# A padded warm-up buffer: 60 bytes that move the buffers behind it

## The chip, the cores and the metric

The kernel runs on one core of a Trainium2 chip. The metric is the device time of one launch in microseconds; times are medians of several runs. The engines of the core run beside each other: TensorE (PE, with its weight loads shown as PEld), VectorE (DVE), ScalarE (ACT), GpSimd (POOL) and SyncE (SP), which here issues nearly all DMA transfers.

## The reference, cut to what matters

Two blocks, one behind the other: a recurrent attention over 768 positions for 4 batches and 8 heads of width 64, and a gated feed-forward block on its 3072 rows.

```python
for t in range(S):                       # attention, per batch and head
    state = gamma * state + einsum('bhd,bhe->bhde', k[:, :, t], v[:, :, t])
    y[:, :, t] = scale * einsum('bhd,bhde->bhe', q[:, :, t], state)
x = y.transpose(0, 2, 1, 3).reshape(3072, 512)
g, val = x @ w_gate, x @ w_val           # 512 x 1536 each
out = (silu(g) * val) @ w_out            # 1536 x 512
```

## The kernel before

The 3072 rows are done in four segments of 768 (s = 0 to 3). Each segment has an up-projection (x times the gate and value weights) and a down-projection (times w_out). The attention that makes the next segment's x runs in pieces of small matmuls (line 766) inside the down-projection of the segment before. Every operand of the large products is split into three parts of lower precision, which VectorE, ScalarE and GpSimd write (`near_a`, `near_b`, `near_c` at lines 967, 970, 973, and `far_a` to `far_c` at 976, 979, 983; where `both` is used in place of `pool`, line 407), and the products of the parts are summed in PSUM.

The large matmuls stand at four lines, each with a weight operand (stationary, 128 x 128) and a moving operand:

- L914 and L896 (`plain_part`, `plain`): up-projection of segment 0. Weights in `oitem` tiles, moving operand x0 of 256 or 384 columns. 144 and 480 matmuls.
- L1062 (`product`, called by `up3`): up-projection of segments 1 to 3, by a scheme with seven products for eight. The weights come in groups, two in `gitem` tiles and one in an `oitem` tile; the moving operand is `xa` or `xb`, 384 columns. 1512 matmuls, six (three parts, two blocks) for each product.
- L1125 (`down`): down-projection of all segments, 12 feature blocks f in each. Stationary operand is the split hidden block `hs[f]`, a `gitem` tile; moving operand is the split w_out block `wo[f]`, an `oitem` tile, 512 columns. 864 matmuls, 18 for each f.

In L1062 and L1125 both operands of one matmul are read from on-chip memory; all matmuls write PSUM banks.

`item(kind, n)` hands out the tiles. The kind "g" has four slots used in turn (tags g0 to g3, 9216 bytes a partition), the kind "o" three (tags o0 to o2, 6144 bytes). Slot g2 is also used once for an `oitem` of segment 0. The pool lays a tag down when it is first asked for, in this order: hT, xa, xb, g0, g1, g3 (as `rawp`), loads, tmp, chunk_x, tab, local, last, states, warm, and behind them o0, o1, o2 and g2. In the built program warm starts at byte 200,960 of each partition, the o slots at 201,504, 207,648 and 213,792, and g2 at 219,936; hT, xa (x0), xb (first), g0, g1, g3, loads, tmp and chunk_x start at 16,512, 53,376, 90,240, 117,888, 127,104, 136,320, 145,536, 168,064 and 178,304.

`warm` is a buffer of 128 + 1 float32 columns. It is set to zero on VectorE (line 1229); one column of it takes a Silu on ScalarE, so that the function's table is loaded early (line 1230); and eight matmuls on its zeros (`warm_up`, line 1214) run while the first inputs are on their way. Nothing reads it afterwards.

The order of the instructions is written out by hand in the string `PLAN`: each word is one step (so `0/D3.1` is segment 0, down-projection, f = 3, output block 1), and `run` issues them in that order. Waits between engines follow from the tiles.

Of the kernel before, what the change touches and what calls it, by code (L numbers as in the profile page):

```python
# [14 lines left out]
AF = mybir.ActivationFunctionType  # L15
ALU = mybir.AluOpType

P = 128
# [358 lines left out]
def tile_retnet_swiglu(  # L377
# [13 lines left out]
    nc = tc.nc  # L391
# [17 lines left out]
    def place(name, n, dtype=F32, **kw):  # L409
        return consts.tile([P, n], dtype, name=name, **kw)  # L410
# [15 lines left out]
    local = place("local", 2 * NP * HC + H + NP)  # L426
    last = place("last", 512)
    states = consts.tile([P, 2, 2, NP, D], F32, name="states")
    warm = place("warm", P + 1)

    def lay(sizes):
        at, out = 0, []
# [778 lines left out]
    def warm_up(n):  # L1211

        for _ in range(n):
            nc.tensor.matmul(banks[3][:, :P], warm[:, :P], warm[:, :P], start=True, stop=True,
                             skip_group_check=True)
# [11 lines left out]
    for n in range(2):  # L1227
        load_chunk(n, 1, nc.scalar)
    nc.vector.memset(warm, 0.0)
    nc.scalar.activation(warm[:, P:], warm[:, :1], AF.Silu)  # L1230
    warm_up(8)
    for f in range(NF):
        up(f, T0 + UP0 * (f - NPF))
# [67 lines left out]
```

## Time and profile before

| what | value |
| --- | --- |
| runs | 657.35, 659.65, 660.76 us; median 659.65 |
| profiled execution: its span from first to last instruction | 655.4 us |
| around that span, median of the runs less the span | 4.25 us |
| TensorE, VectorE, ScalarE, GpSimd busy in the profile | 642.4, 490.1, 389.9, 270.0 us |
| L1062: matmuls, busy | 1512, 292.8 us |
| L1125: matmuls, busy | 864, 212.9 us |
| L896 and L914: matmuls, busy | 624, 104.2 us |
| granted TensorE clock | 1.00 |

The profiled execution's own time is known by its span; what lies around the span is only known from the runs. Busy times of single matmuls overlap, since they are pipelined, so the number of us that a row of n matmuls adds to the span is read from the distance of its start to the next row's start, not from its busy time. Buffer numbers are left out of the profile's names: `gitem` is any of the four slots.

### The profile page before, as it was taken

What the parts mean: (1) busy time and instruction counts of PE and PEld (TensorE: products, weight loads), DVE (VectorE), ACT (ScalarE), POOL (GpSimd) and SP (SyncE); (2) the same over time, 40 slices, a digit from 0 to 9 for tenths busy, and PEclk for the clock granted to TensorE, in tenths of its full rate; (3) what the DMA queues carried; (4) which work ended last, traced back from release to release, by engine and by line L of the source; (5) the groups of instructions that cost most, each with busy time, mean ns of one, the idle gap of its engine ahead of it and who ended that gap; (6) DMA issues with size and microseconds to landing.
All of it is one profiled execution on the core that took longest, in us unless ns stands there. A gap on an engine that the chain in (4) does not pass through costs nothing.

```text
span 655.4 us, 14042 instructions
## 1 busy us (share of the span) xinstructions
PE 642.4 (98%) x5576; PEld 582.5 (89%) x5576; DVE 490.1 (75%) x712; ACT 389.9 (59%) x860; POOL 270.0 (41%) x174
## 2 busy tenths in 40 slices
PE   7999999999999999999999999999999999999997
PEld 6899999987779999997778999998777999999886
DVE  5888688798998887675787868767498776778361
ACT  4688788577855555665766555455676554554211
POOL 1443446533445675630103765640103766562000
PEclk9999999999999999999999999999999999999999
DMA  9999897499867444177765640448677434304554
GB/s 331 372 354 337 316 347 265 165 367 282 280 206 292 162 145 170 33 225 253 235 231 209 214 141 23 164 160 294 193 247 260 165 140 169 114 0 162 184 201 146
DMA packets 50051, 140.13 MB, mean 214 GB/s; under 512 B 4929, under 2 KB 17473, under 8 KB 49985
## 3 DMA queue, kind: packets, MB, share of 16 engines
q1 hardware_dynamic: 49552, 138.57, 61.2%
q8 instruction: 44, 0.72, 0.4%
q10 hardware_dynamic: 432, 0.66, 0.3%
q14 instruction: 23, 0.18, 0.1%
HBM read 109.32 MB, written 29.88 MB: 212 GB/s over the span
## 4 chain that ended last, share of the span: by engine, by line
PE 86%; DVE 5%; DMA 3%; ACT 3%; issue 1%; POOL 1%; SPq 0%; ACTq 0%; DVEq 0%; POOLq 0%
PE bank L1062 40%; PE bank L1125 26%; PE bank L896 12%; PE bank L766 5%; PE bank L914 2%; DMA rawp<-in_w_gate_dram 1%; ACT chunk_x L996 1%; DMA hT<-in_k_n_dram 1%; DVE gitem L970 1%; DMA hT<-in_q_t_dram 1%; DVE oitem L983 1%; POOL oitem L973 1%; DVE gitem L407 0%; DVE xa L983 0%; PE bank L721 0%
## 5 line engine op out<-in xcount | busy, mean ns | idle before, releaser
L1125 PE MATMUL bank<-oitem,gitem 128*128 128x512 f32 x864 | 212.9, 400 | 2.3 <-DVE oitem L983 1.3
L1125 PEld LDWEIGHTS bank<-oitem,gitem 128*128 128x128 f32 x864 | 159.4, 188 | 41.5 <-DVE oitem L983 3.1
L973 POOL TENSOR_TENSOR gitem<-gitem 128x768 fp32r<-128x768 f32 x72 | 143.3, 1999 | 107.1 <-DVE gitem L970 102.3
L1062 PE MATMUL bank<-xa,gitem 128*128 128x384 f32 x864 | 163.0, 337 | 0.6 <-ACT tmp L1078 0.3
L1062 PEld LDWEIGHTS bank<-xa,gitem 128*128 128x128 f32 x864 | 151.3, 188 | 3.0 <-ACT tmp L1077 2.1
L973 POOL TENSOR_TENSOR oitem<-oitem 128x256 fp32r<-128x256 f32 (+1 forms) x60 | 65.8, 1102 | 72.8 <-DVE oitem L970 70.8
L970 DVE SCALAR_TENSOR_TENSOR gitem<-gitem,loads 128x768 fp32r<-128x768 f32 x72 | 80.7, 1138 | 14.1 <-ACT gitem L967 11.6
L967 ACT ACTIVATE gitem<-loads 128x768 fp32r<-128x768 f32 x72 | 59.3, 842 | 51.4 <-PE bank L1062 40.7
L896 PE MATMUL bank<-x,oitem 128*128 128x384 f32 x480 | 86.1, 340 | 0.8 <-POOL oitem L973 0.8
L896 PEld LDWEIGHTS bank<-x,oitem 128*128 128x128 f32 x480 | 84.5, 188 | 1.4 <-POOL oitem L973 1.1
L1062 PE MATMUL bank<-xb,gitem 128*128 128x384 f32 x432 | 85.5, 335 | 0.2 <-POOL gitem L973 0.2
L1062 PEld LDWEIGHTS bank<-xb,gitem 128*128 128x128 f32 x432 | 76.0, 188 | 1.1 <-POOL gitem L973 0.5
L970 DVE SCALAR_TENSOR_TENSOR gitem<-gitem,hT 128x768 fp32r<-128x768 f32 x48 | 51.0, 1067 | 28.4 <-ACT gitem L967 28.3
L967 ACT ACTIVATE gitem<-hT 128x768 fp32r<-128x768 f32 x48 | 39.9, 840 | 43.1 <-PE bank L1125 35.8
L996 ACT COPY chunk_x<-bank 64x128 f32<-64x128 f32 x144 | 35.4, 260 | 29.9 <-PE bank L766 25.4
L793 POOL TENSOR_TENSOR loads<-loads,tab 128x512 f32<-128x512 f32 x9 | 13.8, 1534 | 93.5 <-PE bank L766 93.5
L407 DVE SCALAR_TENSOR_TENSOR gitem<-gitem 128x768 fp32r<-128x768 f32 x48 | 45.9, 962 | 0.6
L1062 PE MATMUL bank<-xb,oitem 128*128 128x384 f32 x216 | 44.3, 340 | 0.0
L1062 PEld LDWEIGHTS bank<-xb,oitem 128*128 128x128 f32 x216 | 38.3, 188 | 0.4 <-POOL oitem L973 0.2
L970 DVE SCALAR_TENSOR_TENSOR oitem<-oitem,loads 128x256 fp32r<-128x256 f32 (+1 forms) x42 | 32.6, 781 | 3.8 <-ACT oitem L967 3.7
L979 POOL TENSOR_TENSOR oitem<-oitem 128x512 fp32r<-128x512 f32 x12 | 20.0, 1667 | 28.4 <-ACT oitem L976 28.4
L1079 DVE TENSOR_TENSOR hT<-bank,tmp 128x384 f32<-128x384 f32 x36 | 20.0, 554 | 15.0 <-PE bank L1062 14.8
(112 smaller groups left out, 785.0 us busy)
## 6 DMA issues: line engine op xcount, KB each, us to landing
loads<-wup SPq DMA_DIRECT2D x36, 896.0 KB, 4.8
oitem<-wdnt SPq DMA_DIRECT2D x36, 768.0 KB, 4.3
wdnt<-oitem SPq DMA_DIRECT2D x12, 768.0 KB, 4.7
wup<-first SPq DMA_DIRECT2D x9, 896.0 KB, 6.7
rawp<-in_w_gate_dram SPq DMA_DIRECT2D x12, 512.0 KB, 6.7
rawp<-in_w_val_dram SPq DMA_DIRECT2D x12, 512.0 KB, 5.9
rawp<-in_w_out_dram SPq DMA_DIRECT2D x12, 512.0 KB, 5.9
out_dram<-chunk_x SPq DMA_DIRECT2D x22, 256.0 KB, 2.2
```

What stands on the lines that cost most here:

```text
L407: stt(o, x, 1.0, y, op0=mul, op1=op)
L766: nc.tensor.matmul(o, a, b, start=start, stop=True, skip_group_check=True)
L793: (pool if i else both)(t, t, qdec, op=mul)
L896: nc.tensor.matmul(o, w[:, a, ts(b, P)], X0[:, a, i, NC - 1 - b], start=a == b == 0, stop=a == 2 and b == NC - 1, skip_group_check=True)
L967: act(o[0], x, AF.Copy, scale=CUT / FAR)
L970: stt(o[1], f32(o[0]), -FAR, x, op0=mul, op1=add)
L973: op(o[2], f32(o[0]), f32(o[1]), op=add)
L979: op(o[1], f32(o[0]), x, op=sub)
L996: copy(cx[half[i], ds(2 * h, 2), c, half[z]], y.rearrange("p (b t) -> p b t", b=2))
L1062: nc.tensor.matmul(o, w[:, a, k], x[:, a, KH - 1 - k], start=start and a == k == 0, stop=a == 2 and k == KH - 1, skip_group_check=True)
L1079: lambda: copy(p5, wb), lambda: tt(h1, x, p5, op=add),
L1125: nc.tensor.matmul(banks[tok], hs[f][:, a, ds(i * TH + u * P, P)], wo[f][:, a], start=f == a == 0, stop=f == NF - 1 and a == 2, skip_group ...
```

## The change

The warm buffer gets 15 more columns (516 to 576 bytes a partition). The Silu reads its one column as before and writes one column, as before. Nothing else in the source is different, and each engine's instructions stand in the same order; the memset of warm is 128 x 144 in place of 128 x 129. In the built program warm stays at 200,960 and what lies behind it moves up by 32 bytes: o0, o1, o2 to 201,536, 207,680 and 213,824, g2 to 219,968.

```diff
-    warm = place("warm", P + 1)
+    warm = place("warm", P + 16)
...
     nc.vector.memset(warm, 0.0)
-    nc.scalar.activation(warm[:, P:], warm[:, :1], AF.Silu)
+    nc.scalar.activation(warm[:, ds(P, 1)], warm[:, :1], AF.Silu)
     warm_up(8)
```

## The prediction

> **What bounds the kernel now.** I read the page's busy times first, then the chain of waits, then the timeline of TensorE, then single stretches of the last stage.
>
> From the page, engine shares and the granted clock in 40 slices:
>
> ```profile
> PE 642.4 (98%) x5576; PEld 582.5 (89%) x5576; DVE 490.1 (75%) x712; ACT 389.9 (59%) x860; POOL 270.0 (41%) x174
> ...
> PEclk9999999999999999999999999999999999999999
> ```
>
> TensorE is busy nearly always, at full clock. The chain that ended last, in pieces (start, us, what), shows whether this is also the path:
>
> ```profile
> 31.70 14.60 PE bank L914 x120
> 46.29 61.48 PE bank L896 x348
> ...
> 216.27 73.48 PE bank L1062 x416
> ...
> 358.62 85.21 PE bank L1062 x486
> ...
> 602.05 49.56 PE bank L1125 x213
> ```
>
> The three up-projections (L1062), the first one (L914, L896) and nearly all down-projections (L1125) are matmuls that follow each other without a wait. Only from 147.7 to 197.8 us, in the first down-projection, does the chain run mostly through VectorE and ScalarE. So the spacing of matmul starts is what the time is made of, and the question is whether that spacing depends on the address of an operand.
>
> It does. The built program puts xa, xb, gitem slots 0, 1 and 3 and all else that TensorE reads at multiples of 64 bytes; the three oitem slots and gitem slot 2 lie at 32 past one. I call these the shifted slots. TensorE's timeline in the third segment's up-projection (start us, us, engine, line, out<-in, count; a row begins where its first matmul starts):
>
> ```profile
> 372.07 1.20 PE L1062 MATMUL bank<-xb,gitem 128*128 128x384 f32 x6
> 373.12 1.20 PE L1062 MATMUL bank<-xa,gitem 128*128 128x384 f32 x6
> 374.16 1.23 PE L1062 MATMUL bank<-xb,oitem 128*128 128x384 f32 x6
> 375.22 3.31 PE L1062 MATMUL bank<-xa,gitem 128*128 128x384 f32 x18
> 378.37 2.24 PE L1062 MATMUL bank<-xb,gitem 128*128 128x384 f32 x12
> 380.45 1.23 PE L1062 MATMUL bank<-xb,oitem 128*128 128x384 f32 x6
> 381.51 3.32 PE L1062 MATMUL bank<-xa,gitem 128*128 128x384 f32 x18
> ```
>
> From start to start, six matmuls with aligned weights take 1.04 us (373.12 to 374.16; twelve take 2.08 from 378.37), and six with weights in oitem take 1.06. The two rows of 18 take 3.15 and 3.17: the first has 6 of its matmuls on gitem slot 2, the second (to 384.68) has 12.
>
> In the last down-projection gitem item f lies in slot f mod 4, so f = 6 alone of these four neighbours has slot 2. Stretches of exactly one f each, 18 matmuls (window, length, PE busy; the x19 counts the one that runs over the edge):
>
> ```profile
> 622.14:626.36 4.22, 4.22 (x19) 3.39 (x18) 1.00 0.74 265
> 626.36:630.45 4.09, 4.09 (x19) 3.38 (x18) 1.00 0.58 192
> 630.45:634.67 4.22, 4.22 (x19) 3.39 (x18) 1.00 0.58 186
> 634.67:638.88 4.21, 4.21 (x19) 3.39 (x18) 1.00 0.53 187
> ```
>
> Here the moving operand is a shifted oitem in all four, and the f whose stationary operand is shifted too is the faster: 227 against 234 ns a matmul. So a shifted place is not dear in itself. What costs is that the two operands sit differently in their 64 bytes; both at 0 or both at 32 is cheap.
>
> **The change part by part.** The warm buffer grows from 516 to 576 bytes a partition. Allocation goes by 32 bytes, so everything behind it moves up by 32: the three oitem slots from 201,504 on and gitem slot 2 (219,936) become multiples of 64. It still fits. No engine's order changes.
>
> *Directly:* the memset of warm writes 144 instead of 129 columns. It takes 0.166 us now (L1229), in proportion 0.185. TensorE does wait for it at 0.8 us, but what follows is warm-up, and the first piece of the chain that is real work hangs on input loads that land at 5.6 and 12.6 us. Cost zero; uncovered, 0.02 us.
>
> *ScalarE, VectorE, GpSimd:* the same operation on slot 2 and on the other gitem slots can be compared. Medians over single instructions, other slots first: L967 from loads 846 and 848 ns, L407 951 and 952, L970 from hT 952 and 954. L973 has its minimum at 1833 and 1832, with medians of 1849 and 1906 that overlapping work spreads. Nothing to gain or lose. *DMA:* packets into or out of oitem (6144 bytes) take 234 ns in the median; those of 4096 and 7168 bytes, at aligned places, 159 and 272, and the line through them gives 234. Zero too.
>
> *TensorE,* from the starts of all successive matmuls of a line (pairs with a wait, over 260 ns, left out; over 200 ns for L914):
> - L1062: 540 matmuls have shifted weights (216 oitem, 324 gitem slot 2) beside aligned xa or xb. Spacing 177.0 ns against 173.7 for the others: 540 x 3.25 = 1.75 us.
> - L896: 480 with shifted weights, 176.8 ns; against the 173.7 of the same width, 480 x 3.1 = 1.5 us.
> - L914: 144 of 256 columns, all shifted, 119.9 ns; no aligned one exists. Scaled from 173.7 by columns 115.8: up to 144 x 4.1 = 0.6 us. I take it whole, since 115 ns is seen among them.
> - L1125: 648 with only the moving operand shifted, 233.9 ns; 216 with both, 229.7. Two aligned operands are not in the trace at this width. The nearest row is the both-shifted one: 648 x 4.2 = 2.7 us. By columns from 173.7 it would be 231.6 ns for all: 648 x 2.3 - 216 x 1.9 = 1.1 us. At the 227.3 ns of the fastest stretch above, 648 x 6.6 + 216 x 2.4 = 4.8 us. I take 2.7, from the same line and width, and keep 1.1 and 4.8 for the range.
>
> Sum 6.5 us; with the ends of L1125, 4.9 to 8.6. Off the path: about 110 of L1125's 648 lie between 147.7 and 197.8 us where the chain is not TensorE's: -0.45. What is late next: TensorE's waits are all small today (the longest behind the start are 0.9 us, each once), but GpSimd and VectorE still have to deliver the operands: in the first up-projection VectorE is busy 78.7 of 97.9 us, in the second GpSimd 58.7 of 90.3. They have room, yet a wait or two of the size seen (0.8 on POOL's oitem, 0.9 on DVE's) will come back: -0.6. That leaves 5.4 to 5.5 us. The profiled execution's span is 655.4, so 649.9 after. The median of the runs is 4.25 above the span; I carry that over: 654.2.
>
> **The rivals.**
>
> *A, the address matters but not in its 64 bytes: no change.* The shifted slots differ from the others in a second thing: they are the only operands of these lines above byte 201,000; the rest lie below 168,000. If pairs in one region are quick and pairs across regions slow, all rows above come out just the same, and a move by 32 bytes does nothing: 659.65. Nothing in this trace separates the two. Against it: in L1062, shifted weights cost 175.3 ns in blocks that start at 288 past a multiple of 1024 and 178.6 at 800, in the same region, so low address bits do count. The Trainium skill (SBUF — State Buffer, Specifications) gives 16-byte cachelines, and 32 past 64 starts such a line as well as 64 does; its section Who interferes with whom gives TensorE two independent read ports, for the moving operand and for weights. By these the spacing would depend on neither address, and the change would bring nothing, 659.65; the 227 against 234 ns speak against the rule as a full account.
>
> *B, the gain is eaten by supply.* TensorE gets faster by the sum, and the operands of the hand-written order come late: each segment's handover (211.3 to 216.3 us, where the chain runs ACT, DVE, POOL gitem) and stage 0 with VectorE at 80% keep their length. If all of stage 0's gain (L896, L914 and its L1125: about 2.7 us) and a few waits go, 2.5 us remain: 657.1. For it: 147.7 to 197.8 is such a stretch already. Against: unbroken pieces of 348, 416 and 486 matmuls on the chain.
>
> *C, slower: the period is 128 bytes.* After the change oitem lies at 64 past a multiple of 128 while xa, xb and gitem 0, 1, 3 lie at 0: the pairs are 64 apart instead of 32. No pair of that distance exists in the trace. If the cost follows the distance in a period of 128 bytes, 64 is the farthest; at twice the price of 32 the 6.1 us on the path are paid once more: 665.8. It decides as soon as a pair 64 apart costs more than one 32 apart, that is over 177.0 ns at 384 columns or 233.9 at 512. For it: 175.3 against 178.6 above says that larger strides than 64 matter. Against: aligned weights at 128 and at 640 past 1024 both take 173.7.
>
> **How the numbers follow.** The forecast (gain of 4 to 8 us realised) 0.63, A 0.15, B 0.12, C 0.10. The forecast's own range is 651.5 to 656. To leave out no more than 2 in 10 the range must take in B and A with most of the runs' spread around it (657.35 to 660.76): 651.5 to 660.4. It leaves out C and the tails. What a measurement of this kernel can tell from no change is about 0.5%, 3.3 us, which puts the bounds at 656.35 and 662.95. Faster: nearly all of the forecast, a third of B, a little of A: 0.67. Slower: C and a tail of the forecast's mechanism at work the other way: 0.11. Same: 0.22.
>
> **What would show it.** Right: six matmuls of L1062 take 1.04 us with oitem as with gitem, L896 spaces at 174 ns, and one f of the last down-projection takes the same in all four slots, 4.09 to 4.17 us. The piece of 348 matmuls of L896 shrinks from 61.5 towards 60.4 us. A shows as unchanged rows with slot 2 still the odd one; B as these rows quicker with longer waits of TensorE for POOL or DVE; C as 1.08 us for six matmuls on oitem and about 4.3 us for an f. A time over 660.4 means that the 64-byte reading of the rows was wrong.

## The result and the profile after

The changed kernel takes 655.88 us in the median of six runs (655.18 to 658.29), the kernel before 658.64 (657.21 to 660.76); the ratio is 0.9965 with a 95% interval from 0.9949 to 0.9981. It is faster by 2.8 us, half of the 5.45 us that the prediction's sum gave. The time is inside the range, which reached up to 660.4 to take in the rivals; the forecast's own case was a gain of 4 to 8 us, and 2.8 is less than the 3.3 us that it took for the least that could be told from no change, though the interval is clear of 1.

The two spans in the profiles, 655.4 and 654.2 us, differ by less than that, for two reasons. Each run's time lies 1.7 to 1.9 us above its own span, so the profiled execution of the kernel before took about 657.2 us, 1.4 less than the median (the 4.25 us that the prediction carried over as lying around the span held such a difference too). The other reason is in the profile after:

```profile
PE 640.8 (98%) x5576; PEld 580.7 (89%) x5576; DVE 490.0 (75%) x712; ACT 389.8 (60%) x860; POOL 271.4 (41%) x174
...
PEclk8999999999999999999999999999999999999999
```

In this execution the granted clock is lower in the first slice: TensorE waited 2.4 us for a load of hT in the start-up, and the clock was 0.5 from 10.9 to 17.8 us. That is not the change's doing: another execution of the same program (after_again below) waited 2.7 us for the same load and had a clock of 1.00 there, as the profile of before has. The pieces of the chain show the start-up apart from the rest:

```profile
33.25 13.80 PE bank L914 x120
47.05 60.32 PE bank L896 x348
...
216.21 73.28 PE bank L1062 x416
...
600.96 49.49 PE bank L1125 x213
```

L914's 120 matmuls begin at 33.25 instead of 31.70 us. From there to the end of the span it was 623.7 us and is now 621.0, 2.7 us less (how far this figure can be trusted is taken up behind the experiments). L896's 348 went from 61.48 to 60.32, L914's 120 from 14.60 to 13.80; but L1062's 416 only from 73.48 to 73.28, and L1125's 213 from 49.56 to 49.49.

TensorE's timeline in the third segment's up-projection, the same products as in the prediction:

```profile
372.77 1.20 PE L1062 MATMUL bank<-xa,gitem 128*128 128x384 f32 x6
373.81 1.21 PE L1062 MATMUL bank<-xb,oitem 128*128 128x384 f32 x6
374.86 3.31 PE L1062 MATMUL bank<-xa,gitem 128*128 128x384 f32 x18
378.01 2.27 PE L1062 MATMUL bank<-xb,gitem 128*128 128x384 f32 x12
380.11 1.21 PE L1062 MATMUL bank<-xb,oitem 128*128 128x384 f32 x6
381.15 3.31 PE L1062 MATMUL bank<-xa,gitem 128*128 128x384 f32 x18
```

The six with weights in oitem now take 1.04 to 1.05 us, as forecast. The rows of 18 take 3.15 (3.15 and 3.17 before), where three times 1.04 would be 3.12; and the row of 12, which had 2.08 with slot 3, now takes 2.10 (378.01 to 380.11): an aligned gitem slot got slower. And the last down-projection, the same four f (5 to 8):

```profile
621.01:625.21 4.20, 4.20 (x19) 3.38 (x18) 1.00 0.74 268
625.21:629.32 4.11, 4.11 (x19) 3.38 (x18) 1.00 0.60 191
629.32:633.52 4.20, 4.20 (x19) 3.38 (x18) 1.00 0.51 187
633.52:637.72 4.20, 4.20 (x19) 3.38 (x18) 1.00 0.53 187
```

Here all operands are at multiples of 64 now, and still slot 2 (f = 6) is the odd one, the sign that the prediction named for rival A.

Mean spacing of matmul starts, worked out from the starts of all matmuls of a line as in the prediction, with d = (address of the moving operand less that of the weights) modulo 256:

```
line, weights             before: d, ns     after: d, ns
L896   oitem              96   176.8        64   173.5
L914   oitem              96   119.9        64   114.0
L1062  oitem, slot 2      96   177.0        64   173.8
L1062  slots 0, 1, 3       0   173.7         0   174.8
L1125  slots 0, 1, 3     160   233.9       192   233.2
L1125  slot 2              0   229.7         0   229.8
```

### The profile page after: what moved, and what is told of

It reads as the page before. It is cut to its first block, busy times and chain, and to the rows that moved or that the text cites. A ratio compares the mean times of both kernels' runs of the same rounds, so it can differ in the third digit from the quotient of the medians.

```text
span 654.2 us, 14042 instructions
## 1 busy us (share of the span) xinstructions
PE 640.8 (98%) x5576; PEld 580.7 (89%) x5576; DVE 490.0 (75%) x712; ACT 389.8 (60%) x860; POOL 271.4 (41%) x174
## 4 chain that ended last, share of the span: by engine, by line
PE 87%; DVE 6%; ACT 2%; DMA 2%; issue 1%; POOL 1%; SPq 0%; ACTq 0%; DVEq 0%; POOLq 0%
PE bank L1062 40%; PE bank L1125 25%; PE bank L896 12%; PE bank L766 5%; PE bank L914 3%; ACT chunk_x L996 1%; DMA rawp<-in_w_gate_dram 1%; DVE gitem L970 1%; PE bank L721 1%; PE bank L636 1%; PE bank L692 1%; DVE oitem L983 1%; PE bank L707 1%; DVE gitem L407 1%; DVE xa L983 1%
## 5 line engine op out<-in xcount | busy, mean ns | idle before, releaser
L1125 PE MATMUL bank<-oitem,gitem 128*128 128x512 f32 x864 | 212.6, 399 | 2.8 <-DVE oitem L983 1.9
L1125 PEld LDWEIGHTS bank<-oitem,gitem 128*128 128x128 f32 x864 | 159.3, 188 | 41.8 <-DVE oitem L983 3.8
L1062 PE MATMUL bank<-xa,gitem 128*128 128x384 f32 x864 | 162.5, 337 | 0.6 <-ACT tmp L1078 0.3
L1062 PEld LDWEIGHTS bank<-xa,gitem 128*128 128x128 f32 x864 | 150.9, 188 | 2.9 <-ACT tmp L1077 2.1
L1062 PE MATMUL bank<-xb,gitem 128*128 128x384 f32 x432 | 85.9, 336 | 0.2 <-POOL gitem L973 0.2
L896 PE MATMUL bank<-x,oitem 128*128 128x384 f32 x480 | 84.6, 337 | 0.8 <-POOL oitem L973 0.8
L896 PEld LDWEIGHTS bank<-x,oitem 128*128 128x128 f32 x480 | 82.9, 188 | 1.5 <-POOL oitem L973 1.1
L1062 PEld LDWEIGHTS bank<-xb,gitem 128*128 128x128 f32 x432 | 76.5, 188 | 1.1 <-POOL gitem L973 0.6
L970 DVE SCALAR_TENSOR_TENSOR gitem<-gitem,hT 128x768 fp32r<-128x768 f32 x48 | 49.1, 1027 | 28.1 <-ACT gitem L967 28.0
L1062 PE MATMUL bank<-xb,oitem 128*128 128x384 f32 x216 | 43.7, 338 | 0.0
L1062 PEld LDWEIGHTS bank<-xb,oitem 128*128 128x128 f32 x216 | 37.8, 188 | 0.4 <-POOL oitem L973 0.2
```

The source lines that it names most:

```text
L896: nc.tensor.matmul(o, w[:, a, ts(b, P)], X0[:, a, i, NC - 1 - b], start=a == b == 0, stop=a == 2 and b == NC - 1, skip_group_check=True)
L970: stt(o[1], f32(o[0]), -FAR, x, op0=mul, op1=add)
L1062: nc.tensor.matmul(o, w[:, a, k], x[:, a, KH - 1 - k], start=start and a == k == 0, stop=a == 2 and k == KH - 1, skip_group_check=True)
L1125: nc.tensor.matmul(banks[tok], hs[f][:, a, ds(i * TH + u * P, P)], wo[f][:, a], start=f == a == 0, stop=f == NF - 1 and a == 2, skip_group ...
```

## The experiments

The theories: the prediction's (only the relative place of the two operands in 64 bytes counts); rival A (a region: the shifted slots are the only operands above byte 201,000); a relative place in a longer period, which is half of rival C; and that weights at 32 past 64 cost time by themselves.

**m1_pairs: pairs of places by themselves.** Six tiles in three regions; each line of its source runs 24 matmuls on one pair.

```diff
+    mm(512, wmid, 0, xhig, 0, 24)      # columns, weights, offset, moving, offset (floats), count
+    mm(512, wmid, 0, xhig, 16, 24)
+    mm(512, whig, 8, xhig, 0, 24)
...
```

> This kernel leaves the whole computation out: it runs matmuls on zeros alone, 24 for each pairing of a weight tile and a moving tile, each from one of three regions (low 53-72 thousand bytes, mid 118-137 thousand, hig 201-220 thousand) and with start offsets of 0, 32, 64 bytes and some finer ones, at 384 and 512 columns; it writes zeros out. What is read is the spacing of starts for each pairing. Theory of the prediction (only the relative place in 64 bytes counts): about 173.7 ns at 384 columns and 230 at 512 whenever both offsets agree modulo 64, 177 and 234 whenever one is at 32 and the other at 0, in all nine pairs of regions alike. Rival 1 (a weight block at 32 past 64 costs 3 ns by itself, and the moving operand's place does not count): 177 wherever the weights have offset 32, also with the moving operand at 32. Rival 2 (region: the 4 ns of line 1125 come from weights in the mid region with a moving operand in the hig one): at 512 columns 233 for weights mid and moving hig at every offset, 230 for both hig. Rival 3 (neither operand's address counts; what differs in the real kernel is other traffic): one value for each width, within 1 ns.

Stretches of exactly one pair each at 512 columns (window, length, PE busy and count): low weights with low moving tile; mid weights with a high moving tile at offset 0, then at 64; then both high at offsets (weights, moving) 0 and 0, 32 and 0, 32 and 32, 64 and 0.

```profile
242.66:248.15 5.49, 5.49 (x25) 4.51 (x25) 0.00 (x0) 0.00 (x0) 1.00 0.01 3
409.11:414.70 5.59, 5.59 (x25) 4.51 (x24) 0.00 (x0) 0.00 (x0) 1.00 0.00 0
437.08:442.56 5.48, 5.48 (x25) 4.50 (x24) 0.00 (x0) 0.00 (x0) 1.00 0.00 0
509.02:514.49 5.47, 5.47 (x25) 4.50 (x24) 0.00 (x0) 0.00 (x0) 1.00 0.01 3
514.49:520.09 5.59, 5.59 (x25) 4.51 (x24) 0.00 (x0) 0.00 (x0) 1.00 0.00 0
525.68:531.16 5.48, 5.48 (x25) 4.51 (x24) 0.00 (x0) 0.00 (x0) 1.00 0.00 0
531.16:536.76 5.60, 5.60 (x25) 4.51 (x24) 0.00 (x0) 0.00 (x0) 1.00 0.00 0
```

The mid tiles start at 128 past a multiple of 256, the high ones at 64. So the second row has d = 192 and is slow; the third shifts the moving tile by 64, d = 0, and is fast, in the same two regions. The last row has both tiles in one region, both at multiples of 64, d again 192, and is as slow as a shift by 32. At this width there is no region, and 64 is not the period. At 512 columns all 54 pairs follow d alone: 226.6 to 227.9 ns a matmul (mean of the last 19 spacings) at d = 0, 228.9 to 229.1 at 64, and 232.5 to 234.3 at the six others, of which 128 is the lowest. Weights at 32 cost nothing where the moving tile is at 32 too (525.68). With no other engine at work, all rivals by other traffic fall as well.

At 384 columns the prediction's theory wanted 177 ns for the 18 pairs with one tile shifted by 32 and the other not: 14 of them took 173.2 to 174.0 and four 176.5 to 176.7. Both tiles at multiples of 64 but 128 apart took 175.5 to 176.2.

Three things do not fit a rule by d alone. At 384 columns d = 32 gave 173.2 ns in most places but 176.5 with the weights at 96 and the moving tile at 128 past a multiple of 256. At the same width d = 160 gave 173.3 and 173.4 in its three places here, but 176.8 in the table of m2_period below. And with offsets that are no multiple of 32 bytes, d = 240 gave 226.7 ns with the moving tile shifted and 233.2 with the weights shifted.

**v128: equal places modulo 256.** One number of the changed kernel.

```diff
-    warm = place("warm", P + 16)
+    warm = place("warm", P + 32)
```

> The warm buffer gets 160 columns instead of 144, so that the oitem slots and gitem slot 2 start at multiples of 128 (128 past a multiple of 256, like gitem 0, 1, 3, xa and xb). If the period is 128 bytes, so that the change left oitem and the other gitem slots 64 apart in line 1125: that line falls from 233.2 to 230 ns a matmul for 648 of them, 2 us less than the changed kernel, about 653.8 us, or 0.992 of the kernel before. If the period is 64 bytes and the rest of line 1125's difference is one of region or of something else: as the changed kernel, 0.9965 of the kernel before, with line 1125 at 233 for slots 0, 1, 3 and 230 for slot 2.

653.08 us (652.40 to 654.30) against 658.39 for the kernel before in the same comparison: 0.9923, interval 0.9908 to 0.9938. The four f of the last down-projection, f = 5 to 8:

```profile
618.78:622.86 4.08, 4.08 (x19) 3.38 (x18) 1.00 0.80 277
622.86:626.94 4.08, 4.08 (x19) 3.38 (x18) 1.00 0.62 193
626.94:631.02 4.08, 4.08 (x19) 3.38 (x18) 1.00 0.58 193
631.02:635.10 4.08, 4.08 (x19) 3.38 (x18) 1.00 0.56 193
```

All four slots are alike now; L1125 stands at 228.2 ns for all slots, L896 at 173.5, L1062's slots 0, 1 and 3 back at 173.7. L914 is at 120 ns as it was before the change. The kernel with one more step of padding beats both.

**o_only and g2_only: the two halves of the change.**

```diff
-    warm = place("warm", P + 16)
+    warm = place("warm", P + 16); [o slots are laid down here]; place("gap", 8); [gitem slot 2]
```

g2_only has P + 1 in place of P + 16 in that line. A gap of 8 floats is 32 bytes.

> Only the three oitem slots are moved to multiples of 64; gitem slot 2 stays at 32 past one (a gap of 32 bytes before it). Phase theory: line 896 at 173.5 and line 914 at 114 ns as in the changed kernel, line 1062 at 173.5 with oitem weights and still 177 with slot 2, line 1125 with slot 2 up from 230 to 234 since now its two operands differ. Region theory for line 1125: slot 2 stays at 230 there. Time: about 0.997 of the kernel before either way, since segment 0 keeps its gain.

656.98 us, 0.9978 (0.9966 to 0.9990). L896 173.5 ns, L914 117.8 (114 was expected), L1062 174.2 with oitem, 176.8 with slot 2 (weights at 96 and moving operand at 128 past a multiple of 256, d = 32: the odd place of m1_pairs, 176.5). L1125 with slot 2 rose from 229.7 to 232.9 ns.

> Only gitem slot 2 is moved to a multiple of 64; the oitem slots stay at 32 past one. Both theories: lines 896 and 914 as before the change (176.8 and 119.9 ns), line 1062 at 173.5 with slot 2 and 177 with oitem. Phase theory: line 1125 with slot 2 rises from 230 to 234 ns, as with the other slots. Region theory: it stays at 230. Time: 0.999 to 1.001 of the kernel before.

658.21 us, 1.0000 (0.9991 to 1.0009). L896 176.8, L1062 173.7 with slot 2 and 177.3 with oitem. L1125 with slot 2 rose to 232.8 ns.

In o_only oitem moves by 32 bytes and slot 2 by 64 (to 220,000), so that it keeps its 32 past a multiple of 64; in g2_only slot 2 moves alone. In both, L1125 on slot 2 has d = 224 and loses its low spacing. That is a pair effect in the full kernel. The alignment of slot 2 by itself is worth nothing: 324 x 3.3 = 1.1 us won in L1062, 216 x 3.1 = 0.7 lost in L1125, and 972 x 0.4 = 0.4 lost in L1062's slots 0, 1 and 3, which rose from 173.7 to 174.2 ns.

**m2_period: the period, and changes of tile.**

```diff
+    mm(512, wlow, 0, xlow, 8, 24)       # d = 0 to 480 in steps of 32 bytes, at 256, 384, 512 columns
...
+    mm(384, wlow, 0, xlow, 16, 6)       # then six and six, with d = 64 and d = 0 in turn
+    mm(384, wmid, 16, xlow, 16, 6)
```

> This kernel leaves the whole computation out and runs matmuls on zeros: first 24 for each difference (address of the moving tile less that of the weight tile, modulo 512) from 0 to 480 in steps of 32, at 256, 384 and 512 columns; then six with one weight tile and six with another in turn, the second at another difference; then the two weight tiles in turn from matmul to matmul. Theory now (difference modulo 256 bytes): rows at d and d + 256 agree at 512 columns within 0.5 ns, about 227 at 0, 229 at 64, 232 to 234 at all others; at 256 columns 113 to 114 at 64 and 120 at 0, as line 914 had in the changed and in the v128 kernel. The theory of the prediction (modulo 64) expects 0, 64, 128 and 192 to be equal at every width. For the blocks in turn: with both tiles at equal differences the average is the plain one; with unequal ones each change of tile costs 10 to 25 ns more, as the 185 and 182 ns in line 1062 of the changed kernel suggest; if those came from other traffic, there is no such cost here.

At 512 columns, stretches of 24 matmuls with d = 0, 32, 64, 96, 128, 192 and 256:

```profile
129.43:134.88 5.44, 5.44 (x25) 4.51 (x25) 0.00 (x0) 0.00 (x0) 1.00 0.00 0
134.88:140.48 5.60, 5.60 (x25) 4.50 (x24) 0.00 (x0) 0.00 (x0) 1.00 0.02 3
140.48:145.98 5.50, 5.50 (x25) 4.51 (x24) 0.00 (x0) 0.00 (x0) 1.00 0.00 0
145.98:151.59 5.61, 5.61 (x25) 4.51 (x24) 0.00 (x0) 0.00 (x0) 1.00 0.00 0
151.59:157.19 5.60, 5.60 (x25) 4.50 (x24) 0.00 (x0) 0.00 (x0) 1.00 0.00 0
162.81:168.41 5.60, 5.60 (x25) 4.49 (x24) 0.00 (x0) 0.00 (x0) 1.00 0.01 3
174.01:179.47 5.46, 5.46 (x25) 4.51 (x24) 0.00 (x0) 0.00 (x0) 1.00 0.00 0
```

The whole table, mean of the last 19 spacings in ns:

```
d (bytes)        0     32     64     96    128    160    192    224
256 columns  120.0  117.7  117.8  119.6  118.6  117.4  113.3  118.3
  d + 256    119.8  117.6  117.7  119.6  118.6  117.4  113.4  118.2
384 columns  173.4  173.4  173.3  176.7  176.2  176.8  174.5  174.0
  d + 256    173.9  173.3  173.4  176.8  176.1  176.8  174.5  174.0
512 columns  226.7  233.3  228.9  233.7  233.5  234.3  233.3  233.3
  d + 256    226.9  233.3  228.9  233.7  233.5  234.3  233.4  233.3
```

With the weights kept in place, the spacing repeats after 256 bytes at all three widths. The large terms of the kernels have the table's values: before, L1062 and L1125 at d = 96 and 160 with 177.0 and 233.9 ns; after, at 64 and 192 with 173.8 and 233.2. Three do not: slot 2 in o_only (above); L914 in the first profile of the changed kernel, 114.0 ns at d = 64 (117.8 in the table, and 117.4 to 117.8 in the other runs with this d); and L1125 on slot 2, 229.7 and 229.8 ns at d = 0 where the table has 226.7. For the last, the 18 spacings of f = 6 in the changed kernel's last down-projection show a part: the first six, behind f = 5 on another slot, are 229 to 236 ns, the others 226 or 227. In v128, where d does not change, all are 226 or 227. The expectation for 256 columns was wrong: the low spacing lies at d = 192, not at 64.

Blocks of six in turn, 36 matmuls of 384 columns; first both tiles at d = 64, then d = 64 and 0, then 64 and 192:

```profile
218.61:224.85 6.24, 6.24 (x37) 6.24 (x36) 0.00 (x0) 0.00 (x0) 1.00 0.01 3
224.85:231.17 6.32, 6.32 (x37) 6.32 (x37) 0.00 (x0) 0.00 (x0) 1.00 0.00 0
231.17:237.45 6.28, 6.28 (x37) 6.28 (x37) 0.00 (x0) 0.00 (x0) 1.00 0.00 0
```

In the second row each d is among the fastest alone, but each of the three changes from d = 64 to 0 costs 27 ns: the last spacing of the old tile is 177 or 178, the next 185, 176, 181 or 182. The change back costs nothing. The same run of numbers, 177, 185, 176, 182, stands in the changed kernel's L1062 where weights go from oitem or slot 2 (d = 64) to slots 0, 1 or 3 (d = 0). There are some 50 such changes, 50 x 27 = 1.35 us by this price; in the mean of slots 0, 1 and 3 (173.74 to 174.76 ns) it is 972 x 1.0 = 1.0 us, since the first of the four raised spacings counts for the old tile. In the kernel before the same changes go from d = 96 to 0 and cost nothing: the spacings behind them are 173.5 ns in the mean. In v128 all weights have the same d, and the 185s of slots 0, 1 and 3 fall from 52 to 10. The last part, two tiles in turn from matmul to matmul, gave 232 ns for either tile at d = 0 and 192 and does not tell which of the two loads is slowed.

**all_32, x64, after_again: what divisibility is worth.**

```diff
-    hT = consts.tile([P, NF, 2, TH], F32, name="hT")          # all_32
+    place("gap", 8); hT = consts.tile([P, NF, 2, TH], F32, name="hT")
-    warm = place("warm", P + 16)
+    warm = place("warm", P + 32)
```

```diff
+    first = place("first", XB, tag="xb"); warm = place("warm", P + 48)      # x64
...
+    [o slots and gitem slot 2 are laid down here]; tab = place("tab", NTAB)
-    warm = place("warm", P + 16)
```

> A gap of 32 bytes before everything and a warm buffer of 160 columns: no large buffer is at a multiple of 64 bytes any more, and all that lines 896, 914, 1062 and 1125 read lie at 160 past a multiple of 256. Theory of the difference modulo 256: as v128, 0.9923 of the kernel before and 653.1 us, with lines 1125 at 228 and 896 at 173.5 ns. Theory that divisibility by 64 (or 128) is what counts: slower than the changed kernel, at or above the kernel before, with line 1062 at 177 ns throughout.

653.45 us, 0.9932 (0.9915 to 0.9949). No large buffer is at a multiple of 64 bytes, and it is as fast as v128: L1125 228.1 ns, L896 173.5, L1062 173.7.

> The changed kernel once more, beside the two above on one chip: 0.9965 of the kernel before, slower than all_32 by 2 to 3 us if the difference modulo 256 decides; not slower than all_32 if divisibility by 64 does.

656.33 us, 0.9969 (0.9958 to 0.9981), 2.9 us slower than all_32 beside it. The spacings are those of the first profile but for L914, which has 117.4 ns here and had 114.0 there, in the same program. What decides between these two stays open.

> The warm buffer with 176 columns stands before the gitem slots, and the oitem slots and gitem slot 2 right behind chunk_x, so that all weight tiles and oitem lie at 64 past a multiple of 256 while xa, xb stay at 128: difference 64 for lines 896, 914 and 1062, 0 for line 1125. Theory of the difference modulo 256: line 1125 at 228, 896 and 1062 at 173.5 as in v128, and line 914 at 114 instead of 120 ns, 144 x 6 = 0.9 us less than v128, 0.991 of the kernel before. Region theory (mid and high places): no gain of line 1125 in particular for slot 2, which now lies with the oitem slots 30 thousand bytes lower. If the gain at 256 columns is hidden: as v128, 0.9923.

653.84 us, 0.9930 (0.9909 to 0.9951): not to be told from v128. L1125 stands at 228.0, L896 at 173.5, L1062 at 173.4 for all weights; L914 at 117.8 instead of 114, so only 144 x 2 = 0.3 us of the 0.9 could be won, less than these runs can tell. The o slots and slot 2 lie 14 thousand bytes lower here (not 30, as the expectation has it), and L1125 does not mind.

## Why the prediction was right, and where its sum was off

**That addresses decide the spacing, and by their relation:** right. All of m1_pairs, o_only and g2_only say so. **That only the place in 64 bytes counts:** wrong; the table repeats after 256 bytes, and equal places modulo 64 are not equal in it. That the next two terms came out all the same was luck: weights moved by 32 bytes went from d = 96 (176.7 ns at 384 columns) to 64 (173.3), while 128, which is as good by the prediction's rule, has 176.2. Of the three signs named for being right, two came (1.04 us in L1062, 173.5 ns in L896); the third, the same time for all four slots in L1125, did not.

**L1062's shifted weights, 1.75 us:** right, 177.0 to 173.8 ns is 540 x 3.2 = 1.7. **L896, 1.5 us:** 480 x 3.3 = 1.6. **L914, 0.6 us:** 144 x 5.9 = 0.85 in the first profile, 0.35 in the second; scaling by columns gave 115.8, and no width has such a rule (113.3 to 120 in the table).

**L1125, 2.7 us:** wrong, this is the term that failed: 648 x 0.7 = 0.45. "The nearest row is the both-shifted one" took a pair at equal places (d = 0) as what two multiples of 64 would do (and its 229.7 ns held a price for the changes of slot too: with equal slots, in v128, it is 228.2). The change put oitem at 64 and left three gitem slots at 128 past a multiple of 256, d = 192, which the table prices at 233.3. The two differ "in their 64 bytes" no longer, but the bytes that count are 256. The lower end that was kept for this term, 1.1 us, was still too high.

**A term that the sum did not have:** the slots that do not move get slower, since changes of weight tile from d = 64 to d = 0 cost 27 ns each: +1.0 us in L1062.

**What is late next, 0.6 us:** right in place, and too small. The same wait of TensorE in the profile before, the profile after and the second profile of the changed kernel (after_again); the numbers are the total in us, the times and the longest:

```profile
PE bank L1125 <- DVE oitem L983: 1.3, 2, 0.9
PE bank L1125 <- DVE oitem L983: 1.9, 2, 1.5
PE bank L1125 <- DVE oitem L983: 2.7, 2, 1.5
```

Counted from the start of L914's 120 matmuls, the first matmul of L1125 starts 2.3 us earlier than before in the profile after and 1.7 in after_again. When segment 1 begins (the first start of L1062), 1.6 and 0.7 of that are left; in v128 0.1 of 1.5. In between lies the stretch that VectorE sets. Counted from the start of the span, segment 1 begins at nearly the same time in the profiles before and after, though L914's 120 had begun 1.55 us later in the second:

```profile
201.77 9.47 PE bank L1062 x54
201.69 9.41 PE bank L1062 x54
```

The off-path share of L1125 shrank with the term, to 0.1.

**Together.** By the spacings and waits of the profile after: 1.7 + 1.6 + 0.85 + 0.45 - 1.0 - 0.6 - 0.1 = 2.9 us, where its pieces from L914 on gave 2.7. That the medians gave 2.8 as well is partly chance: in after_again, the same program, the stretch from L914 on is only 1.7 us shorter than before (622.1 against 623.75), and the medians of that comparison differ by 1.8 (656.33 against 658.17). The part behind segment 0 is firm. From the first start of L1062 to the end of the span it was 453.8 us before and is 452.7 and 452.8 in the two profiles of the changed kernel, and the terms there give 1.7 - 1.0 + 0.3 = 1.0 (0.3 is L1125's share outside segment 0). The rest of the medians' gain lies in the start-up and segment 0. o_only, whose stretch from L1062 on is 453.8 us as before, gained 1.4 us in its median there alone. How that part comes about is open: executions of one program differ there by as much (L914's 120 begin at 33.2 and 32.5 us in the two profiles of the changed kernel).

**Memset, other engines, DMA at nothing:** nothing contradicts it. VectorE, ScalarE and GpSimd are busy for 490.0, 389.8 and 271.4 us (490.1, 389.9 and 270.0 before).

**Rival A (region, no change):** falls by m1_pairs: the 512-column rows at 409.11 and 437.08 differ in the moving tile's offset alone. The rule of the Trainium skill set beside it (SBUF — State Buffer, Who interferes with whom: two independent read ports of TensorE) does not cover what is seen: with no other engine at work, 226.7 against 233.3 ns at 512 columns depend on where both operands lie.

**Rival B (supply):** its first part happened in good measure: between L914 and segment 1, 0.6 of 2.3 us went in one profile of the changed kernel and 1.0 of 1.7 in the other. In the later up-projections TensorE had no longer waits; there the gain was lost in spacing.

**Rival C (longer period, slower):** its premise, a longer period, was right (256 bytes, not 128) and its price wrong. At 512 columns 64 apart (d = 192) costs what 32 apart costs (d = 32 and 224), 233.3 ns in the table, not twice, and which way round matters: d = 64 is 228.9. At 384 columns d = 64 costs nothing, and that carried the terms of L896 and L1062.

## What to carry to other kernels

Where matmuls follow each other without a gap and every one loads new weights, the place of the moving operand relative to the weights can cost 2 to 3% of the spacing (173.3 to 176.8 ns at 384 columns, 226.7 to 234.3 at 512); compare the spacings of starts by buffer slot before asking for a rule of alignment. A pair of slots seen in the trace prices only the difference that it has: here equal places modulo 256 bytes were the safe choice at 384 and 512 columns, and multiples of 64 were not the point (all_32 has none and is as fast as v128). When one operand comes from several slots in turn, give all of them the same place, since the change itself had a price.

## What the runs showed of the hardware that was not expected

- With the weights in one place, the spacing repeats when the moving operand goes 256 bytes further, at 256, 384 and 512 columns, within 0.5 ns; and it is not symmetric (d = 64 and 192 at 512 columns: 228.9 and 233.3).
- Which difference is best depends on the width: 192 at 256 columns (113.3 against 120.0 at 0), 0 at 512 (226.7 against up to 234.3).
- At 384 columns a change of weight tile between two fast differences cost 27 ns in one direction (d = 64 to 0) and nothing in the other.
- At 384 columns places with equal difference were not always equal (173.2 and 176.5 at d = 32, 173.3 and 176.8 at d = 160), so the difference is not the whole rule; what else enters was not settled.
